# A planner's weights for VectorE work beside an attention stream: 99 pairs of quarter tiles become 103

## Chip, cores, metric

One NeuronCore of one Trainium2 chip runs the whole kernel. The metric is the device time of one execution in microseconds; the kernel before is given as the median of three runs, and one further execution was profiled.

## The reference, cut to what matters

The kernel computes two branches on the same input and mixes them with a gate per row:

```python
g = sigmoid((x * gate_w).sum(-1, keepdims=True))       # x: 1 x 2048 x 1024
a = state_space_branch(x)      # h[t] = Lam_bar * h[t-1] + Bu[t]; y = 2 Re(h C^T) + x * Dskip
qkv = x @ wqkv                 # 32 heads of 32
p = softmax(q @ k.T * 32 ** -0.5)
b = (p @ v) @ wo
out = g * a + (1 - g) * b
```

What matters here is the softmax: 32 heads x 2048 x 2048 exponentials have to be taken of scores that lie in PSUM.

## The kernel before, in words

**The stream.** The attention is cut into 8 groups of 4 heads, each group into 8 units of 256 queries, and each unit into 8 bursts (`BURSTS`): 512 bursts p = 0 to 511, unit U = p // 8. A burst (`burst`, L1613) is 8 score matmuls on TensorE (L1625), which fill two PSUM tiles of 128 x 1024, and two exponentials on ScalarE, `exp(0)` and `exp(1)`, one per tile (L1644). There are three such PSUM tiles, used in turn. The exponentials of a burst are multiplied with V some bursts later (`pv`, L1728) and summed in one PSUM bank, called "O". When the last burst of a unit has been summed, in burst 8U + 9, `normalize` (L1735) has VectorE take the reciprocal of the sums (L1741) and scale the result (L1742), and only then may the next unit's sums start in that bank. Everything else (projections, the state space branch, the output projection) is cut into chains of matmuls that are fed to TensorE, four to a burst ("dense" work), each chain ending with an evacuation by VectorE.

**The quarter tiles.** In some bursts ScalarE takes only 768 of the 1024 columns of the second tile (L1641), and VectorE takes the other 256. VectorE copies them scaled out of PSUM (`x_in`, L1634, 128x256). Two bursts make a pair, and for a pair VectorE then runs three steps of a polynomial over 128x512 (L1668, L1669, L1665, listed in `x_ops`, L1654); GpSimd turns the result into bf16 bits (`x_p`, L1666), and TensorE multiplies that with V (`x_pv`, L1695; its matmuls are L1707). `X_PLAN` (L937) lists where pairs lie. A unit with two pairs has them in its bursts (0, 2) and (4, 6); a unit with one pair has it in (0, 4). `x_plan` (L1648) sets when the result is multiplied, in `x_when`: in burst 8U + 7 for a pair (0, 2), in burst 8U + 9 for the others. I call that burst the due burst. The matmuls L1707 stand in TensorE's queue behind the values of earlier bursts and in front of that burst's dense matmuls and of all score matmuls of later bursts.

**The planner.** All queues are in order, and their order is written when the program is built. For each burst, `build` (L1753) keeps a model of VectorE's clock, `dve_t`, and a limit for the burst. The loop from L1926 on fills the room up to the limit with steps of three lists: `xbg` (the steps of pairs), `bg` (the state space items: 8 tensor_tensor and two scans each, `item_ops`, L1343) and `bg2` (tables and folds). It tries every number i of pair steps, j of item steps and k of table steps that fit, takes the best value, and issues the first step of that choice. `mixed` (L1672) says how long a choice takes and which step leads: it changes lists where it can, since a step right behind one of its own list costs `DEP` more. Before the change the value is

```python
v = (u + (0.3 * i if ended is not None else 9.0 * i) + 0.05 * sum(x[0] for x in bs[:j]), i, j, k, lead)
```

with u the time that the choice takes, and `ended` set where a dense chain ends in this burst. So in a burst without an evacuation, pair steps come first whenever they fit. If the steps of a pair are not all issued when its due burst comes, `values` (L1831) calls `x_flush` (L1689), which issues them there.

Of the kernel before, what the change touches and what calls it, by code (L numbers as in the profile page):

```python
# [927 lines left out]
PE_HEAD = 0.86  # L928
# [5 lines left out]
W_AT = (38, 0, 17)  # L934

X_AT = ((0, 2), (4, 6), (0, 4))
X_PLAN = (64, 72, 80, 88, 92, 96, 100, 104, 108, 112, 116, 120, 124, 128, 132, 136, 144, 152, 160, 168, 172, 176, 180, 184, 188, 192, 200, 208, 216, 224, 228, 232, 236, 240, 244, 248, 252, 256, 260, 264, 268, 272, 276, 280, 284, 288, 292, 296, 300, 304, 308, 312, 316, 320, 324, 328, 332, 336, 344, 348, 352, 356, 360, 364, 368, 372, 376, 380, 384, 388, 392, 396, 400, 404, 408, 412, 416, 420, 424, 428, 432, 436, 440, 444, 448, 452, 456, 460, 464, 468, 472, 476, 480, 484, 488, 492, 496, 500, 504)  # L937
X_COLS = 256
F_TS, F_ST = 1.32, 1.24
DEP = 0.12  # L940
I_MM = 0.6
X_LAST = 0.615
U_LAG, U_AHEAD = 3, 32
LATE, LATE0 = 0.35, 0.15
X_A = SCALE * math.log2(math.e) * 65536.0
X_LO = -127.0 * 65536.0
E3, E2, E1, E0 = 0.0780245226404788, 0.2260671649, 0.6958335355, 0.9999252185627155
# [13 lines left out]
class FastPath:  # L961
# [381 lines left out]
    def item_ops(self, j, ch, n):  # L1343
# [9 lines left out]
        def tt(c, o, a, b, op, r, w, d=0.0):  # L1353
            ops.append((c, d, lambda: dve(lambda e: e.tensor_tensor(o, a, b, op), r, w)))
        two = lambda ap: ap.unsqueeze(1).to_broadcast([128, 2, 512])
        tt(I_MM, ht[:], ub[s], two(er), ALU.mult, [u0, u1, Et], k[0:2])
        tt(I_MM, tq[:], ub[s], two(ei), ALU.mult, [u0, u1, Et], k[2:4])
        ops.append((0.0, 0.0, lambda: self.used_u(n)))
        tt(0.61, ut[:, 0, :], t[0], t[3], ALU.add, [k[0], k[3]], [("ut", 0)], DEP)
        tt(0.61, ut[:, 1, :], t[1], t[2], ALU.subtract, k[1:3], [("ut", 1)])  # L1360
# [7 lines left out]
        k = [("tq", 0), ("tq", 1), ("ut", 0), ("ut", 1)]  # L1368
        tt(I_MM, tq[:], ht[:], two(er), ALU.mult, [("ht", 0), ("ht", 1), Et], k[0:2], DEP)
        tt(I_MM, ub16[:, :, 0:512], ht[:], two(ei), ALU.mult, [("ht", 0), ("ht", 1), Et], k[2:4])  # L1370
        (h0, w0), (h1, w1) = self.hp_at(ch, j, 0), self.hp_at(ch, j, 1)
        hw = ["warm"] if ch == 0 and j == 0 else []
        if ch == 1 and j == 0:
            hw = ["fX", "fY", "m_c"] + self.EFtok + ["gp0", "gp1"]
        tt(0.345, h0, t[0], t[3], ALU.subtract, [k[0], k[3]], w0 + hw, DEP)
        tt(0.345, h1, t[2], t[1], ALU.add, k[1:3], w1 + hw)
# [236 lines left out]
    def burst(self, B):  # L1613
# [17 lines left out]
        if mine is not None:  # L1631
            b, n = mine
            s = sl[1]
            first = self.dve(lambda e: e.tensor_scalar(self.xi[:, b % 2, X_COLS * n:X_COLS * (n + 1)], ps[:, 2 * s + 1, 512 - X_COLS:512], X_A, X_LO, ALU.mult, ALU.max),  # L1634
                             [("S", s)], [("xi", b % 2, n)], "x_in")
# [18 lines left out]
    def x_ops(self, b):  # L1654
# [8 lines left out]
        def last():  # L1663
# [3 lines left out]
            self.x_done.add(b)  # L1667
        return [(0.61, DEP, lambda: self.dve(lambda e: e.scalar_tensor_tensor(xq[:], lo, E2 / E3 * w, lo, ALU.add, ALU.mult), i2, ["xq"], "x_q")),  # L1668
                (0.61, DEP, lambda: self.dve(lambda e: e.scalar_tensor_tensor(xq[:], xq[:], E1 / E3 * w * w, lo, ALU.add, ALU.mult), ["xq"] + i2, ["xq"], "x_q")),  # L1669
                (X_LAST, DEP, last)]  # L1670

    def mixed(self, xs, bs, ts):  # L1672

        rest = {"x": list(xs), "b": list(bs), "t": list(ts)}
        t, lane, lead = 0.0, self.lane, ""
        while True:
            some = [s for s in "xbt" if rest[s]]
            if not some:
                return t, lead
            s = next((s for s in some if s != lane), some[0])  # L1680
            if rest["b"] and rest["b"][0][0] == 0.0:
                s = "b"
            c, d = rest[s].pop(0)
            lead = lead or s
            if c > 0:
                t += c + (d if s == lane else 0.0)
                lane = s

    def x_flush(self):  # L1689
        c, d, f = self.xbg.pop(0)  # L1690
        f()
        self.dve_t += c + (d if self.lane == "x" else 0.0)
        self.lane = "x"
# [59 lines left out]
    def build(self):  # L1753
# [45 lines left out]
        outs, k = [], 0  # L1799
# [9 lines left out]
        t0, period = 0.0, PERIOD  # L1809
        for p in range(first, NBURST):  # L1810
# [3 lines left out]
            if p > first:  # L1814
                t0 += period
            if p % 4 == 0 and p in X_PLAN:
                one = p % 8 == 0 and p + 4 not in X_PLAN and p < NBURST - 8
                self.x_plan(p // 8, X_AT[2 if one else p // 4 % 2])
# [3 lines left out]
            period = PERIOD - (0.17 if p - 1 in self.x_of else 0.0)  # L1822
            if p in self.x_of:
                self.dve_t = max(self.dve_t, t0 + 0.45) + 0.4
                b, n = self.x_of[p]
                if n == 1:
                    self.xbg += self.x_ops(b)
                self.lane = "x"
            q0, q1 = self.quarters[p]

# [31 lines left out]
            if not wo1 and not cs and cur is None and self.c_left[3] == 0:  # L1862
                wo1 = True
                for a in range(7):
                    j = a if a < 3 else a - 3
                    x = [("cT", 0, j), ("cTf", 0, j, 0), ("cTf", 0, j, 1)]
                    if a in (3, 4, 5):
                        x = [("bT", a - 3)] + [("hp", 8, k) for k in (2 * a - 6, 2 * a - 5)]
# [11 lines left out]
            ended = None  # L1880
            while used < quota:
                if cur is None:
# [4 lines left out]
                    elif not last:  # L1887
                        nxt = proj[g + 1]
                        left = 64 - pg
                        need = 2 * len(nxt)  # L1890
                        u_ok = c_ok = False
                        if us:
                            ch, n, ri, dn = us[0]
# [16 lines left out]
                wt, f = cur.pieces.pop(0)  # L1910
# [3 lines left out]
                if not cur.pieces:  # L1914
                    ended = cur
# [4 lines left out]
            if behind:  # L1920
                values()
            log.append((p, ended.tag if ended else (cur.tag if cur else None), used, round(self.dve_t - t0, 2), len(self.bg) + len(self.bg2)))
            limit = t0 + period + PE_HEAD
            if ended is not None:
                limit = dense_end + (LATE if behind else LATE0 if period > 1.8 else 0.0)
            while self.xbg or self.bg or self.bg2:  # L1926
                now = max(self.dve_t, t0 + 0.3)
                room = limit - now + 1e-9
                xs, bs = [], []
                for c, d, f in self.xbg:  # L1930
                    if c == X_LAST and self.x_out != len(self.x_done):
                        break
                    xs.append((c, d))
                    if c == X_LAST:
                        break
                for c, d, f, n in self.bg:
                    if not ((n in self.tabled or not self.bg2) and self.item_ready(n)) or sum(x[0] for x in bs) > room:
                        break
                    bs.append((c, d))
                ts = [(c, 0.0) for c, f in self.bg2[:8]]  # L1940
                if not bs and not xs and not ts:
                    break
                best = None
                for i in range(len(xs) + 1):
                    for j in range(len(bs) + 1):
                        if self.mixed(xs[:i], bs[:j], [])[0] > room:
                            break
                        for k in range(len(ts) + 1):
                            u, lead = self.mixed(xs[:i], bs[:j], ts[:k])
                            if u > room:  # L1950
                                break
                            v = (u + (0.3 * i if ended is not None else 9.0 * i) + 0.05 * sum(x[0] for x in bs[:j]), i, j, k, lead)
                            if best is None or v > best:
                                best = v
                lead = best[4]
                if not lead:
                    break
                if lead == "x":
                    c, d, f = self.xbg.pop(0)
                elif lead == "b":  # L1960
                    c, d, f, n = self.bg.pop(0)
                else:
                    (c, f), d = self.bg2.pop(0), 0.0
                f()
                if c > 0:
                    self.dve_t = now + c + (d if self.lane == lead else 0.0)
                    self.lane = lead
# [189 lines left out]
```

## Time and profile before

| what | value |
|---|---|
| time, median of 3 runs (lowest to highest) | 925.74 us (924.91 to 925.8) |
| the profiled execution's own time | 925.63 us |
| its span, first to last instruction | 923.9 us |
| TensorE clock granted | 0.999 |
| VectorE busy | 770.5 us (83%) |
| GpSimd busy | 86.4 us (9%) |
| ScalarE instructions L1641 (768 columns) | 198 |
| GpSimd steps L1666 | 99 |

"Busy" is the union of an engine's instructions. ScalarE's instructions overlap one another at their ends, so the time that one of them really takes from the stream is read from start to start in the timeline. In the view of waits a line reads "who waited <- for whom: us in total, times, longest". In a timeline a row is start, length, engine, line, operation, tiles, count; several like instructions are merged into one row.

### The profile page before, as it was taken

The page shows a single profiled execution, that of the slowest core. Times are in us where ns is not written, and L with a number is a line of the kernel's source. Part 1 is how long each engine was busy: PE and PEld are TensorE (multiplying, and loading weights), DVE is VectorE, ACT ScalarE, POOL GpSimd, SP SyncE. Part 2 cuts the span into 40 slices and gives each one's busy share as a digit, 9 for nine tenths or more (in the row PEclk, how much of TensorE's full clock was granted, in tenths as well). Part 3 has the DMA queues.
Part 4 walks back from the last instruction along what each step waited for, and adds up shares of the span by engine and source line. Part 5 has one row for each costly group of instructions (what it writes and reads, how often), then busy time and mean ns, then how long its engine had stood idle before and what let it go on. Part 6 is the DMA issues. An engine that isn't in the chain of part 4 may idle for free.

```text
span 923.9 us, 34036 instructions
## 1 busy us (share of the span) xinstructions
PE 901.5 (98%) x15316; PEld 503.1 (54%) x15316; DVE 770.5 (83%) x1345; ACT 905.7 (98%) x1034; POOL 86.4 (9%) x163
## 2 busy tenths in 40 slices
PE   8899999999999999999999999999999999999996
PEld 4555744556555565555655565555655655545553
DVE  2788989999989999999999999989998655676665
ACT  6999999999999999999999999999999999999996
POOL 2000001011000101010111110101001010000010
PEclk9999999999999999999999999999999999999999
DMA  9449767630564202242212621622001012534422
GB/s 199 86 101 150 105 116 146 139 83 16 104 118 100 65 20 72 75 97 53 41 41 77 127 50 25 133 65 67 20 22 48 21 60 69 185 85 129 114 62 75
DMA packets 170983, 77.70 MB, mean 84 GB/s; under 512 B 147280, under 2 KB 155472, under 8 KB 170832
## 3 DMA queue, kind: packets, MB, share of 16 engines
q1 hardware_dynamic: 168672, 74.94, 35.7%
q8 instruction: 121, 1.98, 0.9%
q10 hardware_dynamic: 2160, 0.53, 0.3%
q14 instruction: 30, 0.25, 0.1%
HBM read 25.18 MB, written 20.97 MB: 50 GB/s over the span
## 4 chain that ended last, share of the span: by engine, by line
PE 54%; ACT 36%; DVE 5%; SPq 1%; DMA 1%; issue 1%; POOL 0%; DVEq 0%
ACT f_pt L1644 29%; PE f_ps L1728 14%; PE f_ps L1625 11%; PE f_ps L1427 9%; PE f_ps L1505 8%; PE f_ps L1458 6%; PE f_ps L1446 5%; ACT f_pt L1641 5%; SPq L1063 1%; ACT f_cT L1644 1%; DVE f_ht L1363 1%; ACT f_Et L1644 1%; PE f_ps L1707 1%; DMA f_xT<-in_A_x_dram 1%; PE f_ps L1511 0%
## 5 line engine op out<-in xcount | busy, mean ns | idle before, releaser
L1644 ACT ACTIVATE f_pt<-f_ps 128x1024 bf16<-128x1024 f32 x746 | 718.2, 1086 | 2.7 <-PE f_ps L1625 2.3
L1728 PEld LDWEIGHTS f_ps<-f_V,f_pt 128*128 128x128 bf16 x7156 | 220.8, 96 | 96.1 <-issue 69.7
L1728 PE MATMUL f_ps<-f_V,f_pt 128*128 128x33 bf16 x7156 | 257.2, 178 | 0.6 <-ACT f_pt L1644 0.6
L1625 PE MATMUL f_ps<-f_Q,f_K 32*128 32x256 bf16 x4096 | 203.3, 273 | 9.0 <-ACT f_cT L1644 2.2
L1641 ACT ACTIVATE f_pt<-f_ps 128x768 bf16<-128x768 f32 x198 | 176.6, 892 | 0.0
L1625 PEld LDWEIGHTS f_ps<-f_Q,f_K 32*128 32x128 bf16 x4096 | 60.7, 92 | 146.8 <-ACT f_pt L1644 118.5
L1458 PE MATMUL f_ps<-f_xT,f_wb 128*128 128x512 bf16 x512 | 131.5, 379 | 1.3 <-DVE f_pf L1240 0.5
L1666 POOL TENSOR_SCALAR f_xp<-f_xq 128x512 int16<-128x512 f32 x99 | 66.9, 676 | 618.9 <-DVE f_xq L1665 418.5
L1427 PE MATMUL f_ps<-f_xT,f_wb 128*128 128x512 bf16 x464 | 119.3, 379 | 0.4 <-DVE f_Q L1434 0.3
L1634 DVE TENSOR_SCALAR f_xi<-f_ps 128x256 int32<-128x256 f32 x198 | 83.4, 421 | 15.9 <-PE f_ps L1625 11.6
L1363 DVE TENSOR_TENSOR_SCAN f_ht<-f_pf,f_init,f_ut 128x512 bf16<-128x512 f32 x64 | 81.1, 1279 | 0.0
L1505 PE MATMUL f_ps<-f_cT,f_hp 128*128 128x512 bf16 x272 | 74.5, 379 | 0.1
L1669 DVE SCALAR_TENSOR_TENSOR f_xq<-f_xq,f_xi 128x512 f32<-128x512 f32 x99 | 68.5, 692 | 3.3
L1668 DVE SCALAR_TENSOR_TENSOR f_xq<-f_xi 128x512 f32<-128x512 uint16 x99 | 68.5, 692 | 3.3
L1665 DVE SCALAR_TENSOR_TENSOR f_xq<-f_xi,f_xq 128x512 f32<-128x512 int16 x99 | 68.2, 689 | 2.2
L1458 PEld LDWEIGHTS f_ps<-f_xT,f_wb 128*128 128x128 bf16 x512 | 40.1, 96 | 40.3 <-issue 9.1
L1446 PE MATMUL f_ps<-f_wb,f_xT 128*128 128x128 bf16 x896 | 59.3, 219 | 0.0
L1427 PEld LDWEIGHTS f_ps<-f_xT,f_wb 128*128 128x128 bf16 x464 | 36.1, 96 | 35.9 <-issue 7.6
L1446 PEld LDWEIGHTS f_ps<-f_wb,f_xT 128*128 128x128 bf16 x896 | 50.4, 97 | 3.8 <-issue 3.8
L1462 DVE CAST f_ub<-f_ps 128x512 bf16<-128x512 f32 x64 | 44.0, 688 | 9.5 <-PE f_ps L1458 8.6
L1741 DVE RECIPROCAL f_rc<-f_ps 128x8 f32<-128x8 f32 x63 | 13.0, 207 | 40.0 <-PE f_ps L1707 34.5
L1536 PE MATMUL f_ps<-f_cT,f_OT 128*128 128x512 bf16 x156 | 44.7, 378 | 0.1
(149 smaller groups left out, 829.0 us busy)
## 6 DMA issues: line engine op xcount, KB each, us to landing
u_scratch<-f_ub SPq DMA_DIRECT2D x64, 128.0 KB, 2.0
f_ub<-u_scratch SPq DMA_DIRECT2D x32, 256.0 KB, 2.9
ag_scratch<-f_Ag SPq DMA_DIRECT2D x32, 256.0 KB, 2.2
f_hp<-ag_scratch SPq DMA_DIRECT2D x32, 256.0 KB, 3.0
f_wb<-in_B_wqkv_dram SPq DMA_DIRECT2D x21, 256.0 KB, 4.1
out_dram<-f_xT SPq DMA_DIRECT2D x16, 256.0 KB, 2.2
f_cT<-in_B_wo_dram SPq DMA_DIRECT2D x5, 256.0 KB, 5.5
f_OT<-f_On SPq DMA_TRANSPOSE x63, 2.5
```

What stands on the lines that cost most here:

```text
L1363: ops.append((1.2, 0.0, lambda ri=ri: dve(lambda e: e.tensor_tensor_scan(ht[:, ri, :], rr, ut[:, ri, :], self.init[:, ri, j:j + 1], ALU.mu ...
L1427: mms.append((1, lambda e, f, l, a=a, w=w: e.matmul(ps[:, bank, :], w[:, a, :], xT[:, a, 512 * ch:512 * (ch + 1)], start=f, stop=l), [tok] ...
L1446: m = e.matmul(ps[:, bank, 128 * q:128 * (q + 1)], xT[:, a, 128 * kt:128 * (kt + 1)], w[:, a, :], start=(a == 0), stop=(a == 7))
L1458: mms.append((1, lambda e, f, l, a=a: e.matmul(ps[:, 7, :], bT[:, (2 * n + ri) % 3, a, :], xT[:, a, 512 * ch:512 * (ch + 1)], start=f, sto ...
L1505: mms.append((1, lambda e, f, l, j=j, ri=ri, h=h: e.matmul(ps[:, 7, :], h[:, cols], cT[ri][:, j, 512 * cb:512 * (cb + 1)], start=f, stop=l ...
L1625: m = e.matmul(ps[:, 2 * sl[h // 2] + h % 2, 256 * kl:256 * (kl + 1)], K[32 * h:32 * h + 32, g % 2, 128 * kt:128 * (kt + 1)], Q[32 * h:32 ...
L1634: first = self.dve(lambda e: e.tensor_scalar(self.xi[:, b % 2, X_COLS * n:X_COLS * (n + 1)], ps[:, 2 * s + 1, 512 - X_COLS:512], X_A, X_LO ...
L1641: self.S.op("act", lambda e: e.activation(flat(self.tile[p]), flat(ps[:, 2 * s:2 * s + 2, :]), ACT.Exp, scale=SCALE), reads=[("S", s)], wr ...
L1644: self.act(lambda e: e.activation(self.tile[p], ps[:, 2 * s:2 * s + 2, :], ACT.Exp, scale=SCALE), [("S", s)], [("pt", p)], "exp")
L1668: return [(0.61, DEP, lambda: self.dve(lambda e: e.scalar_tensor_tensor(xq[:], lo, E2 / E3 * w, lo, ALU.add, ALU.mult), i2, ["xq"], "x_q") ...
L1669: (0.61, DEP, lambda: self.dve(lambda e: e.scalar_tensor_tensor(xq[:], xq[:], E1 / E3 * w * w, lo, ALU.add, ALU.mult), ["xq"] + i2, ["xq"] ...
L1728: m = e.matmul(ps[:, 6, o:o + 33], self.tile[p][:, h2, 256 * kl + 128 * qt:256 * kl + 128 * (qt + 1)], V[:, g % 2, 2 * i + kl, h, :], star ...
```

## The change

The diff, cut to its core (`X_PLAN` grows by the entries 84, 156, 164 and 220; nothing leaves it):

```diff
+X_SOON, X_LEFT = 0.0, 2
+RC_LATE = 0.25
...
             s = next((s for s in some if s != lane), some[0])
+            if self.hurry and rest["x"]:
+                s = "x"
             if rest["b"] and rest["b"][0][0] == 0.0:
...
                 if n == 1:
-                    self.xbg += self.x_ops(b)
+                    due = 8 * (p // 8) + (7 if p % 8 < 4 else 9)
+                    self.xbg += [(c, d, f, due) for c, d, f in self.x_ops(b)]
...
-            limit = t0 + period + PE_HEAD
+            limit = t0 + period + PE_HEAD + (RC_LATE if p + 1 in self.quarters and self.quarters[p + 1][1] % 32 == 0 else 0.0)
             if ended is not None:
                 limit = dense_end + (LATE if behind else LATE0 if period > 1.8 else 0.0)
...
+                left = next((n for n, x in enumerate(self.xbg) if x[0] == X_LAST), 0) + 1
+                soon = self.xbg and left > self.xbg[0][3] - p - X_LEFT
+                self.hurry = soon and self.xbg[0][3] - p <= 1
...
-                            v = (u + (0.3 * i if ended is not None else 9.0 * i) + 0.05 * sum(x[0] for x in bs[:j]), i, j, k, lead)
+                            w = sum(x[0] for x in xs[:i] + bs[:j] + ts[:k])
+                            v = (w + ((0.3 if ended is not None else 9.0) if soon else X_SOON) * i + 0.05 * sum(x[0] for x in bs[:j]), i, j, k, lead)
```

- **Four more pairs.** Units 10, 19, 20 and 27 had one pair in bursts (0, 4); they now have two, in (0, 2) and (4, 6).
- **Weights.** Each step now carries its due burst. With `left` steps of the first pair open, the extra weight of a pair step counts only where `left` is more than due - p - 2; elsewhere a pair step counts like any other. The value uses w, the plain sum of the costs, in place of u, which held the bubbles between steps of one list too.
- **Hurry.** In the burst ahead of the due burst (and in it), a pair step leads whatever ran just before.
- **The limit.** In the burst ahead of a unit's reciprocal (p = 8U + 8), if no chain ends there, the limit is 0.25 later.

No instruction is of a new kind. The matmul work and the number of exponentials stay as they are.

More of the change, by code (lines that the diff above doesn't have):

```diff
@@ L936 @@
 X_AT = ((0, 2), (4, 6), (0, 4))
-X_PLAN = (64, 72, 80, 88, 92, 96, 100, 104, 108, 112, 116, 120, 124, 128, 132, 136, 144, 152, 160, 168, 172, 176, 180, 184, 188, 192, 200, 208, 216, 224, 228, 232, 236, 240, 244, 248, 252, 256, 260, 264, 268, 272, 276, 280, 284, 288, 292, 296, 300, 304, 308, 312, 316, 320, 324, 328, 332, 336, 344, 348, 352, 356, 360, 364, 368, 372, 376, 380, 384, 388, 392, 396, 400, 404, 408, 412, 416, 420, 424, 428, 432, 436, 440, 444, 448, 452, 456, 460, 464, 468, 472, 476, 480, 484, 488, 492, 496, 500, 504)
+X_PLAN = (64, 72, 80, 84, 88, 92, 96, 100, 104, 108, 112, 116, 120, 124, 128, 132, 136, 144, 152, 156, 160, 164, 168, 172, 176, 180, 184, 188, 192, 200, 208, 216, 220, 224, 228, 232, 236, 240, 244, 248, 252, 256, 260, 264, 268, 272, 276, 280, 284, 288, 292, 296, 300, 304, 308, 312, 316, 320, 324, 328, 332, 336, 344, 348, 352, 356, 360, 364, 368, 372, 376, 380, 384, 388, 392, 396, 400, 404, 408, 412, 416, 420, 424, 428, 432, 436, 440, 444, 448, 452, 456, 460, 464, 468, 472, 476, 480, 484, 488, 492, 496, 500, 504)
 X_COLS = 256
@@ L1689, in x_flush @@
     def x_flush(self):
-        c, d, f = self.xbg.pop(0)
+        c, d, f, due = self.xbg.pop(0)
         f()
@@ L1929, in build @@
                 xs, bs = [], []
-                for c, d, f in self.xbg:
+                for c, d, f, due in self.xbg:
                     if c == X_LAST and self.x_out != len(self.x_done):
@@ L1958, in build @@
                 if lead == "x":
-                    c, d, f = self.xbg.pop(0)
+                    c, d, f, due = self.xbg.pop(0)
                 elif lead == "b":
```

## The prediction

> **What bounds the kernel now.** I read the page first: its span and busy shares, then the two groups of exponentials.
>
> ```profile
> span 923.9 us, 34036 instructions
> PE 901.5 (98%) x15316; PEld 503.1 (54%) x15316; DVE 770.5 (83%) x1345; ACT 905.7 (98%) x1034; POOL 86.4 (9%) x163
> L1644 ACT ACTIVATE f_pt<-f_ps 128x1024 bf16<-128x1024 f32 x746 | 718.2, 1086 | 2.7 <-PE f_ps L1625 2.3
> L1641 ACT ACTIVATE f_pt<-f_ps 128x768 bf16<-128x768 f32 x198 | 176.6, 892 | 0.0
> ```
>
> PE and ACT both show 98%. The group rows show ACT waiting only 2.7 us in front of its 746 main instructions, and not at all in front of the 198 short ones. So ACT is the steady bound, with PE beside it. The waits say which of the two waits for the other:
>
> ```profile
> PEld f_ps L1625 <- ACT f_pt L1644: 118.5, 308, 1.0
> DVE f_rc L1741 <- PE f_ps L1707: 34.5, 38, 1.8
> PEld f_ps L1707 <- POOL f_xp L1666: 2.4, 4, 0.7
> ```
>
> PE waits 118.5 us for ACT before it writes new scores, so in most bursts PE has time to spare. The second row is the gap in front of the reciprocal: VectorE stands idle there, about 0.9 us each (34.5 / 38). The third row is small, but it is the one place where a late quarter tile holds PE's queue: four times, up to 0.7 us. What such a tile is worth on ACT is read from start to start in ACT's timeline, here for a unit with one pair (20) and one with two (21):
>
> ```profile
> 299.65 0.81 ACT L1641 ACTIVATE f_pt<-f_ps 128x768 bf16<-128x768 f32 x1
> 300.36 6.52 ACT L1644 ACTIVATE f_pt<-f_ps 128x1024 bf16<-128x1024 f32 x7
> ...
> 313.72 0.98 ACT L1641 ACTIVATE f_pt<-f_ps 128x768 bf16<-128x768 f32 x1
> 314.50 2.95 ACT L1644 ACTIVATE f_pt<-f_ps 128x1024 bf16<-128x1024 f32 x3
> 317.23 0.93 ACT L1641 ACTIVATE f_pt<-f_ps 128x768 bf16<-128x768 f32 x1
> 317.97 2.94 ACT L1644 ACTIVATE f_pt<-f_ps 128x1024 bf16<-128x1024 f32 x3
> 320.69 0.91 ACT L1641 ACTIVATE f_pt<-f_ps 128x768 bf16<-128x768 f32 x1
> 321.41 2.95 ACT L1644 ACTIVATE f_pt<-f_ps 128x1024 bf16<-128x1024 f32 x3
> 324.13 0.93 ACT L1641 ACTIVATE f_pt<-f_ps 128x768 bf16<-128x768 f32 x1
> 324.86 2.95 ACT L1644 ACTIVATE f_pt<-f_ps 128x1024 bf16<-128x1024 f32 x3
> 327.61 0.91 ACT L1641 ACTIVATE f_pt<-f_ps 128x768 bf16<-128x768 f32 x1
> ```
>
> Three full tiles take 317.23 - 314.50 = 2.73 us, 0.91 each. A short one takes 0.78, 0.74, 0.72 and 0.73 in the four places (0.71 in unit 20).
>
> **Term 1, the four pairs.** Each pair turns two full tiles into short ones. What is new in a unit are the places of bursts 2 and 6: 0.91 - 0.74 and 0.91 - 0.73, together 0.35 us. Four units make **-1.4 us**. Its ends: with the worst place (0.78) 8 x 0.13 = 1.0, with the best (0.71) 8 x 0.20 = 1.6.
>
> VectorE pays for them with two reads of PSUM and three steps a pair:
>
> ```profile
> L1634 DVE TENSOR_SCALAR f_xi<-f_ps 128x256 int32<-128x256 f32 x198 | 83.4, 421 | 15.9 <-PE f_ps L1625 11.6
> L1665 DVE SCALAR_TENSOR_TENSOR f_xq<-f_xi,f_xq 128x512 f32<-128x512 int16 x99 | 68.2, 689 | 2.2
> 690.00:713.00 23.00, 22.50 (x382) 12.10 (x381) 20.70 (x37) 22.44 (x27) 2.47 (x4) 1.00 0.22 54
> 713.00:736.00 23.00, 23.00 (x451) 15.31 (x448) 15.23 (x28) 23.00 (x28) 1.85 (x3) 1.00 0.06 17
> ```
>
> That is 2 x 0.42 + 3 x 0.69 = 2.9 us a pair, 11.6 us in all. (The steps L1668 and L1669 have the shape of L1665.) None of it stands on ACT's path. What hides it is the state space work, which fills VectorE up to 713 us (20.70 of 23 us busy) and then ends (15.23). 11.6 us more move that end back, less what the wider limit gains: at most 0.25 in each of the units 8 to 48, 41 x 0.25 = 10 us. I cost this at nothing. If the cover were gone, the last chunk of matmuls that needs the state space work would come up to 11.6 us later, in TensorE slots that are filled with projections meanwhile; as each is dense work in an existing slot, only the lack of a filler would cost. The new reads of PSUM themselves must be done before ACT's short tile. I take them as free too; if VectorE is behind, their price is what the late one of unit 20 has: it ends at 299.62, and the short tile starts at 299.65, so that the two full tiles from 297.60 on take 2.05 us where 1.82 is normal: 0.23 lost.
>
> ```profile
> 297.60 2.08 ACT L1644 ACTIVATE f_pt<-f_ps 128x1024 bf16<-128x1024 f32 x2
> ...
> 299.20 0.42 DVE L1634 TENSOR_SCALAR f_xi<-f_ps 128x256 int32<-128x256 f32 x1
> ```
>
> Eight new ones at that price would be 2 us, and this is the upper end.
>
> **Term 2, the late steps.** The four waits of PE for POOL look alike. This is the one at burst 288, in order of time, with a punctual one of unit 20 at the end:
>
> ```profile
> 523.29 0.42 DVE L1634 TENSOR_SCALAR f_xi<-f_ps 128x256 int32<-128x256 f32 x1
> 523.62 0.68 DVE L1354 TENSOR_TENSOR f_tq<-f_ht,f_Et 128x1024 bf16<-128x1024 bf16 x1
> 524.22 0.69 DVE L1665 SCALAR_TENSOR_TENSOR f_xq<-f_xi,f_xq 128x512 f32<-128x512 int16 x1
> 524.81 0.37 PE L1728 MATMUL f_ps<-f_V,f_pt 128*128 128x33 bf16 x8
> 524.93 2.03 ACT L1644 ACTIVATE f_pt<-f_ps 128x1024 bf16<-128x1024 f32 x2
> 524.99 0.62 POOL L1666 TENSOR_SCALAR f_xp<-f_xq 128x512 int16<-128x512 f32 x1 [1.95 <-DVE f_xq L1665]
> 525.66 0.27 PE L1707 MATMUL f_ps<-f_V,f_xp 128*128 128x33 bf16 x4 [0.49 <-POOL f_xp L1666]
> ...
> 527.18 1.02 ACT L1644 ACTIVATE f_pt<-f_ps 128x1024 bf16<-128x1024 f32 x1 [0.22 <-PE f_ps L1625]
> ...
> 300.06 0.37 PE L1728 MATMUL f_ps<-f_V,f_pt 128*128 128x33 bf16 x8
> 300.28 0.26 PE L1707 MATMUL f_ps<-f_V,f_xp 128*128 128x33 bf16 x4
> ```
>
> The pair's last step was left for the burst ahead of its due burst. There an item step (f_tq) went in front of it, because the planner changes lists where it can. The matmuls L1707 start 0.85 us behind the values' first matmul, against 0.22 in the punctual row: 0.63 late. The dense chain and the next scores stand behind them, and ACT's two tiles from 524.93 take 2.25 us where 1.82 is normal. So a late step is on the path with most of its length; four make the 2.4 us of the waits row.
>
> The change makes such a step lead. It would start at 523.62 instead of 524.22, 0.60 earlier, and if POOL followed as quickly, L1707 would be 0.03 late and the whole 2.4 us would go. But now f_tq runs right behind the step, beside POOL, and the trace has that case:
>
> ```profile
> 169.78 0.68 DVE L1354 TENSOR_TENSOR f_tq<-f_ht,f_Et 128x1024 bf16<-128x1024 bf16 x1
> 169.94 0.99 POOL L1666 TENSOR_SCALAR f_xp<-f_xq 128x512 int16<-128x512 f32 x1 [1.01 <-DVE f_xq L1665]
> ...
> L1666 POOL TENSOR_SCALAR f_xp<-f_xq x99: 617/618/1591, 139.9 to 906.8; 128x512 int16<-128x512 f32 x99
> ```
>
> Beside f_tq the POOL step takes 0.99 us instead of 0.62, and up to 1.59 elsewhere. Then a hurried step saves only 0.60 - 0.37 = 0.23 us, and four save 0.9. The Trainium skill (GPSIMD Engine Reference, section 8, Key points) speaks against the change in the same sense: GpSimd and VectorE share SBUF interfaces, and a VectorE instruction that reads two SBUF tensors or runs in a 2-port mode gets in GpSimd's way. The trace agrees (0.99 against 0.62 us beside an operation with two SBUF inputs); if the rule holds at all four places, term 2 is the 0.9, not the 2.4.
>
> Whether a last step still falls there depends on a new order of all VectorE work from burst 84 on. For the second pair of a unit the weights hardly change: three steps are left three bursts ahead of the due burst, and 3 > 3 - 2, so they weigh at once as before. For a first pair the weight starts one burst later than before. So I expect about as many late steps, cheaper ones, or fewer. I take the middle of 0.9 and 2.4, **-1.6 us**; the ends are -2.4 and, with as many late steps more, the slower rival below.
>
> **Term 3, the limit.** In busy units VectorE now runs up to 0.25 us into the gap in front of the reciprocal. Where the gap is 0.9 us, this costs nothing. The tightest case has no gap at all:
>
> ```profile
> 202.67 0.20 DVE L1741 RECIPROCAL f_rc<-f_ps 128x8 f32<-128x8 f32 x1
> 202.91 0.42 DVE L1742 SCALAR_TENSOR_TENSOR f_On<-f_ps,f_rc 128x256 bf16<-128x256 f32 x1
> ...
> 203.69 0.36 PE L1728 MATMUL f_ps<-f_V,f_pt 128*128 128x33 bf16 x8
> ```
>
> The scaled result is done at 203.33 and the bank is needed at 203.69, so 0.36 us are left there; 0.25 more still fit, with 0.11 over for the hand-over. The price lies between 0 and, if every one of 41 units lost 0.1, 4 us. I take **+0.2**, near the row, since the planner's steps are 0.6 or 1.2 long and seldom fill the last tenth. Queued behind the reciprocal on VectorE are the scaling, an evacuation and the next read of PSUM; they would shift by the same 0.25.
>
> **Sum.** Against the profiled execution's 925.63 (span 923.9 and 1.7 around it): 925.63 - 1.4 - 1.6 + 0.2 = **922.8 us**. The median of the runs, 925.74, is 0.11 above that execution; I leave it at 922.8.
>
> **Rivals.** The bound for "no change" is 0.2%, 1.85 us, about what a measurement of this kernel can tell; so faster is below 923.9 and slower above 927.6.
> - *All late steps go:* no pair ends in the burst ahead of its due burst. 925.63 - 1.6 - 2.4 - some tenths of the 2.7 us idle = 921.2. For it: the step leads there, and the limit has grown by 0.25. Against it: the POOL row.
> - *The pairs alone:* late steps are moved to other units and cost what they did, 925.63 - 1.4 + 0.2 = 924.4; this is also what comes out if "hurry" does not do what it says. For it: the weights in bursts with an evacuation are the same as before (0.3), and there a scan of 1.2 beats a step.
> - *Reciprocals late:* all of term 3's upper end eats the gain: 925.63 - 1.4 - 1.6 + 4 = 926.6.
> - *Slower, more late steps:* the first pair's later weight pushes its last step into the second pair's time, so that two steps of a second pair are left for the burst ahead of the due burst, or a step is followed by an operation that holds POOL for its longest, 1.59. Each such pair costs about 0.63 + 0.3 = 0.9 us at L1707. It decides the sign when their sum passes 1.4 + 2.4 + 1.85 = 5.7 us, from some six or seven such pairs among about forty in the busy stretch: 928.2 with seven.
>
> **Chances.** Forecast 0.45; all gone 0.17; pairs alone 0.20; reciprocals late 0.06; slower 0.12. Faster holds the first two, 0.62; same the next two, 0.26; slower 0.12. The range goes from 920.8 (term 1 at 1.6, term 2 at 2.4, and 0.8 of the idle) to 926.0, inside the case of late reciprocals; it leaves out the slower rival and the end of that case.
>
> **What would show it.** Term 1: 206 rows of L1641, and units 10, 19, 20 and 27 shorter by 0.35 us. Term 2: PE's wait for POOL at L1707 falls from 2.4 us, and where it stays, the POOL step is longer than 0.62. Term 3: reciprocals wait less for PE than 34.5 us and no L1728 waits for L1742. It is wrong if L1707 waits more than four times at 0.6, or if L1641 shows idle time in front for L1634.

## The result and the profile after

The changed kernel takes 923.76 us (median of 17 runs, 923.08 to 924.54), the kernel before 925.6 (17 runs, 924.65 to 925.94). The ratio is 0.9982, 95% interval 0.9975 to 0.9988: faster by 1.7 us going by the ratio and by 1.84 going by the medians. My bound for "no change" was 0.2%, 1.85 us, so this is at its edge; that it is faster is clear. The profiled execution took 923.76, so the two profiled executions are 1.87 us apart. The line numbers have moved: L1646 and L1643 are the full and the short exponentials, L1667 the last step of a pair, L1668 GpSimd's step, L1711 the pair's matmuls, L1732 the values, L1745 and L1746 the reciprocal and the scaling.

Lines of the changed kernel's page, then some of its waits (who waited <- for whom: us, times, longest), and the line of GpSimd's step before. Here and below only the rows that matter are shown, of timelines too:

```profile
span 921.9 us, 33840 instructions
...
L1646 ACT ACTIVATE f_pt<-f_ps 128x1024 bf16<-128x1024 f32 x738 | 711.9, 1082 | 3.2 <-PE f_ps L1627 3.0
L1643 ACT ACTIVATE f_pt<-f_ps 128x768 bf16<-128x768 f32 x206 | 183.0, 889 | 0.0
L1668 POOL TENSOR_SCALAR f_xp<-f_xq 128x512 int16<-128x512 f32 x103 | 82.8, 804 | 598.7 <-DVE f_xq L1667 423.8
```

```profile
PEld f_ps L1627 <- ACT f_pt L1646: 117.6, 302, 1.0
...
DVE f_rc L1745 <- PE f_ps L1711: 36.2, 38, 1.8
...
PEld f_ps L1711 <- POOL f_xp L1668: 1.7, 3, 0.9
PEld f_ps L1732 <- DVE f_On L1746: 1.5, 7, 0.2
...
DVE f_ht L1356 <- DMA f_ub<-u_scratch: 1.1, 1, 1.1
```

```profile
L1666 POOL TENSOR_SCALAR f_xp<-f_xq 128x512 int16<-128x512 f32 x99 | 66.9, 676 | 618.9 <-DVE f_xq L1665 418.5
```

ScalarE is still the bound, with 206 short tiles. The waits at L1711 went from four (2.4 us) to three (1.7 us), not to none, and GpSimd's step grew from 676 to 804 ns on average. The last of the waits is new: VectorE waits 1.1 us for a load.

**Where the 1.87 us came from.** The gain has two parts that I had foreseen, the tiles of the four pairs and the late steps. A third part appeared in the opening, and a wait for a load took about half of the foreseen gain away.

*The pairs.* ScalarE's timeline at the new short tiles (bursts 2 and 6) of units 10, 19 and 20:

```profile
163.26 0.93 ACT L1643 ACTIVATE f_pt<-f_ps 128x768 bf16<-128x768 f32 x1
164.04 2.90 ACT L1646 ACTIVATE f_pt<-f_ps 128x1024 bf16<-128x1024 f32 x3
...
288.46 0.93 ACT L1643 ACTIVATE f_pt<-f_ps 128x768 bf16<-128x768 f32 x1
289.30 2.86 ACT L1646 ACTIVATE f_pt<-f_ps 128x1024 bf16<-128x1024 f32 x3
...
295.48 0.83 ACT L1643 ACTIVATE f_pt<-f_ps 128x768 bf16<-128x768 f32 x1
296.22 2.88 ACT L1646 ACTIVATE f_pt<-f_ps 128x1024 bf16<-128x1024 f32 x3
...
302.72 0.83 ACT L1643 ACTIVATE f_pt<-f_ps 128x768 bf16<-128x768 f32 x1
303.56 2.85 ACT L1646 ACTIVATE f_pt<-f_ps 128x1024 bf16<-128x1024 f32 x3
...
309.68 0.89 ACT L1643 ACTIVATE f_pt<-f_ps 128x768 bf16<-128x768 f32 x1
310.37 2.94 ACT L1646 ACTIVATE f_pt<-f_ps 128x1024 bf16<-128x1024 f32 x3
```

From start to start: 0.78, 0.84, 0.74, 0.84, 0.69 us. The other place of unit 10 and the two of unit 27 are 0.73, 0.78 and 0.73. Against 0.91 of a full tile the eight save 1.15 us. The two of 0.84 are those of burst 2 in units 19 and 20.

*The late steps.* Seven last steps still lie in the burst ahead of their due burst (due 177, 241, 273, 281, 297, 321, 369). Each leads now. Behind four of them (177, 281, 321, 369) VectorE runs the reciprocal next; there GpSimd's step takes 0.62 us and the four cost hardly anything. The dearest is the one of burst 241:

```profile
438.41 0.68 DVE L1667 SCALAR_TENSOR_TENSOR f_xq<-f_xi,f_xq 128x512 f32<-128x512 int16 x1
439.01 1.28 DVE L1365 TENSOR_TENSOR_SCAN f_ht<-f_pf,f_init,f_ut 128x512 bf16<-128x512 f32 x1
439.18 1.52 POOL L1668 TENSOR_SCALAR f_xp<-f_xq 128x512 int16<-128x512 f32 x1 [3.07 <-DVE f_xq L1667]
439.55 0.37 PE L1732 MATMUL f_ps<-f_V,f_pt 128*128 128x33 bf16 x8
440.76 0.27 PE L1711 MATMUL f_ps<-f_V,f_xp 128*128 128x33 bf16 x4 [0.84 <-POOL f_xp L1668]
442.31 1.02 ACT L1646 ACTIVATE f_pt<-f_ps 128x1024 bf16<-128x1024 f32 x1 [0.70 <-PE f_ps L1627]
```

The step itself came in time. A scan runs right behind it, and beside the scan GpSimd's step takes 1.52 us; L1711 starts 1.21 us behind the values where 0.22 is punctual, and ScalarE stands idle for 0.70. The two other waits (273, 297) have f_tq behind the step and a GpSimd step of 0.99. Less waiting at L1711 is worth 2.4 - 1.7 = 0.7 us.

*The opening.* Before and after, the starts of bursts 40 and 41 on ScalarE (two full tiles lie between):

```profile
84.95 1.94 ACT L1644 ACTIVATE f_pt<-f_ps 128x1024 bf16<-128x1024 f32 x2
87.08 1.94 ACT L1644 ACTIVATE f_Et<-f_ps 128x1024 bf16<-128x1024 f32 x2 [0.19 <-PE f_ps L1625]
```

```profile
84.60 1.94 ACT L1646 ACTIVATE f_pt<-f_ps 128x1024 bf16<-128x1024 f32 x2
86.42 1.95 ACT L1646 ACTIVATE f_Et<-f_ps 128x1024 bf16<-128x1024 f32 x2
```

2.13 us became 1.82. In the kernel before, an item step stood between the scaling and the evacuation of a projection, and TensorE waited for that evacuation. Burst 58 gains as much. Together this is 0.6 us, which I had not foreseen; 0.2 of it is lost again in bursts 60 to 64.

*The load.* At burst 68 of the changed kernel:

```profile
138.04 0.69 DVE L1356 TENSOR_TENSOR f_ht<-f_ub,f_Et 128x1024 bf16<-128x1024 bf16 x1 [1.13 <-DMA f_ub<-u_scratch]
138.13 3.77 ACT L1646 ACTIVATE f_pt<-f_ps 128x1024 bf16<-128x1024 f32 x4
...
140.46 0.69 DVE L1464 CAST f_ub<-f_ps 128x512 bf16<-128x512 f32 x1
...
141.50 0.81 PE L1460 MATMUL f_ps<-f_xT,f_wb 128*128 128x512 bf16 x3 [1.27 <-DVE f_ub L1464]
...
142.69 1.94 ACT L1646 ACTIVATE f_pt<-f_ps 128x1024 bf16<-128x1024 f32 x2 [0.79 <-PE f_ps L1627]
```

The first pair's steps no longer come first there; an item step does, and its input has not landed. VectorE stands for 1.13 us, the evacuation behind it is late, the chain behind the evacuation starts 1.27 late, and ScalarE idles 0.79. From start to start its four tiles take 142.69 - 138.13 = 4.56 us here, where four full tiles elsewhere take 3.63: 0.93 is lost, in burst 70.

*The sum.* Subtract the start of every burst on ScalarE in the one profiled execution from that in the other. Most bursts between 71 and 510 take the same time in both within 0.03 us, so the differences can be put to places. They add up to the 1.97 us between the two spans:

| where | changed less before, us |
|---|---|
| bursts 0 to 39 | -0.35 |
| bursts 40 and 58, the earlier evacuation | -0.60 |
| bursts 59 to 65 | +0.20 |
| burst 70, behind the load | +0.93 |
| units 10, 19, 20 and 27, the new pairs | -1.16 |
| the four late steps of before (185, 289, 329, 385) gone | -2.68 |
| the late steps 241, 273 and 297 of the changed kernel | +1.87 |
| everything else | -0.18 |

The first line is no gain of the change. VectorE's order is the same in both up to 70.8 us (burst 33), and nearly all of the 0.35 arises ahead of that. Two runs below that share the order of the kernel before there reach burst 40 at 84.84 (hurry alone) and 86.42 us (the step ahead of the read) where the kernel before has 84.95. What makes the opening vary by over a microsecond from execution to execution is not shown.

### The profile page after: what moved, and what is told of

The parts are those of the page before. It is cut to its first block, busy times and chain, and to the rows that moved or that the text cites. A ratio compares the mean times of both kernels' runs of the same rounds, so it can differ in the third digit from the quotient of the medians.

```text
span 921.9 us, 33840 instructions
## 1 busy us (share of the span) xinstructions
PE 882.3 (96%) x15095; PEld 503.8 (55%) x15316; DVE 769.6 (83%) x1365; ACT 903.8 (98%) x1034; POOL 101.9 (11%) x167
## 4 chain that ended last, share of the span: by engine, by line
PE 53%; ACT 30%; DVE 13%; issue 2%; DMA 1%; POOL 0%; DVEq 0%; SPq 0%
ACT f_pt L1646 23%; PE f_ps L1732 12%; PE f_ps L1627 10%; PE f_ps L1507 8%; PE f_ps L1429 8%; PE f_ps L1460 6%; PE f_ps L1448 5%; ACT f_pt L1643 5%; DVE f_xi L1636 3%; DVE f_ht L1365 2%; ACT f_cT L1646 1%; DVE f_ub L1464 1%; DVE f_Ag L1520 1%; PE f_ps L1711 1%; DVE f_xq L1670 1%
## 5 line engine op out<-in xcount | busy, mean ns | idle before, releaser
L1646 ACT ACTIVATE f_pt<-f_ps 128x1024 bf16<-128x1024 f32 x738 | 711.9, 1082 | 3.2 <-PE f_ps L1627 3.0
L1732 PEld LDWEIGHTS f_ps<-f_V,f_pt 128*128 128x128 bf16 x7140 | 221.7, 96 | 94.7 <-issue 65.9
L1732 PE MATMUL f_ps<-f_V,f_pt 128*128 128x33 bf16 x7140 | 256.9, 178 | 0.1
L1643 ACT ACTIVATE f_pt<-f_ps 128x768 bf16<-128x768 f32 x206 | 183.0, 889 | 0.0
L1668 POOL TENSOR_SCALAR f_xp<-f_xq 128x512 int16<-128x512 f32 x103 | 82.8, 804 | 598.7 <-DVE f_xq L1667 423.8
L1460 PE MATMUL f_ps<-f_xT,f_wb 128*128 128x512 bf16 x448 | 117.7, 379 | 9.0 <-DVE f_ub L1464 1.7
L1429 PE MATMUL f_ps<-f_xT,f_wb 128*128 128x512 bf16 x406 | 106.7, 379 | 4.1 <-issue 0.4
L1636 DVE TENSOR_SCALAR f_xi<-f_ps 128x256 int32<-128x256 f32 x206 | 86.8, 421 | 25.8 <-PE f_ps L1627 21.5
L1671 DVE SCALAR_TENSOR_TENSOR f_xq<-f_xq,f_xi 128x512 f32<-128x512 f32 x103 | 71.0, 689 | 2.5
L1670 DVE SCALAR_TENSOR_TENSOR f_xq<-f_xi 128x512 f32<-128x512 uint16 x103 | 70.7, 686 | 2.5 <-POOL f_xp L1668 0.7
L1667 DVE SCALAR_TENSOR_TENSOR f_xq<-f_xi,f_xq 128x512 f32<-128x512 int16 x103 | 70.8, 687 | 1.9
L1507 PE MATMUL f_ps<-f_cT,f_hp 128*128 128x512 bf16 x240 | 67.6, 379 | 2.5 <-DVE f_Ag L1520 0.5
L1745 DVE RECIPROCAL f_rc<-f_ps 128x8 f32<-128x8 f32 x63 | 13.0, 206 | 40.5 <-PE f_ps L1711 36.2
L1356 DVE TENSOR_TENSOR f_ut<-f_ht,f_tq 128x512 f32<-128x512 bf16 x64 | 43.0, 691 | 0.6
```

What stands on the lines that cost most here:

```text
L1429: mms.append((1, lambda e, f, l, a=a, w=w: e.matmul(ps[:, bank, :], w[:, a, :], xT[:, a, 512 * ch:512 * (ch + 1)], start=f, stop=l), [tok] ...
L1460: mms.append((1, lambda e, f, l, a=a: e.matmul(ps[:, 7, :], bT[:, (2 * n + ri) % 3, a, :], xT[:, a, 512 * ch:512 * (ch + 1)], start=f, sto ...
L1507: mms.append((1, lambda e, f, l, j=j, ri=ri, h=h: e.matmul(ps[:, 7, :], h[:, cols], cT[ri][:, j, 512 * cb:512 * (cb + 1)], start=f, stop=l ...
L1643: self.S.op("act", lambda e: e.activation(flat(self.tile[p]), flat(ps[:, 2 * s:2 * s + 2, :]), ACT.Exp, scale=SCALE), reads=[("S", s)], wr ...
L1646: self.act(lambda e: e.activation(self.tile[p], ps[:, 2 * s:2 * s + 2, :], ACT.Exp, scale=SCALE), [("S", s)], [("pt", p)], "exp")
L1668: self.pool(lambda e: e.tensor_scalar(bits, xq[:], X_K, 128.0 * (E0 + 126.0), ALU.mult, ALU.add), ["xq"], p2, "x_p")
```

## The experiments

My theory: ScalarE sets the pace; what the plan does to VectorE matters only through the last steps of pairs (by when they come and by what runs on VectorE beside GpSimd's step) and through the one wait for the load. The rivals were that hurry gives all of its 0.6 us, that late steps are made good, that the pairs buy nothing beside a busy TensorE, that the load's wait is absorbed, and that the limit acts by itself. In every run the planned order says how many last steps are late; that is a list read off before the run. The four pairs by themselves could not be tried: with the old weights or the old limit the state space work ends too late for the chains that need it, and no order comes out.

**Hurry alone** (the kernel before, with this only):

```diff
             s = next((s for s in some if s != lane), some[0])
+            if self.hurry and rest["x"]:
+                s = "x"
```

> The kernel before with one part of the change: in the burst ahead of its due burst a pair step leads. The planned order keeps the same four late last steps (due bursts 185, 289, 329, 385), each now right behind the read of PSUM. Theory (GpSimd's step collides with the item step that now runs beside it): the last step is 0.6 us earlier, GpSimd's step takes 0.99 instead of 0.62, TensorE's wait at the pair's matmuls falls from about 0.6 to about 0.4 each, time 925.6 - 0.9 = 924.7. Rival (no collision): GpSimd's step stays at 0.62, TensorE does not wait for it at all, time 925.6 - 2.4 = 923.2.

Measured: 925.3 against 926.06 us, ratio 0.9992 (0.9983 to 1.0001), that is 0.8 us less. The place that the prediction quoted, due burst 289, and the waits of this run:

```profile
523.41 0.68 DVE L1667 SCALAR_TENSOR_TENSOR f_xq<-f_xi,f_xq 128x512 f32<-128x512 int16 x1
524.01 0.68 DVE L1356 TENSOR_TENSOR f_tq<-f_ht,f_Et 128x1024 bf16<-128x1024 bf16 x1
524.17 0.99 POOL L1668 TENSOR_SCALAR f_xp<-f_xq 128x512 int16<-128x512 f32 x1 [1.34 <-DVE f_xq L1667]
524.60 0.37 PE L1732 MATMUL f_ps<-f_V,f_pt 128*128 128x33 bf16 x8
525.23 0.27 PE L1711 MATMUL f_ps<-f_V,f_xp 128*128 128x33 bf16 x4 [0.26 <-POOL f_xp L1668]
```

```profile
PEld f_ps L1711 <- POOL f_xp L1668: 1.5, 4, 0.4
```

All four GpSimd steps take 0.99, as worked out: the step leads, and f_tq takes most of that back. The wait fell from 2.4 to 1.5. The time alone doesn't settle it (its interval reaches 1.0001); the rows do. Apart from these four places VectorE's order is that of the kernel before, and from start to start ScalarE gains 0.23 us at each of them, 0.9 in all.

**The step ahead of the read.** In place of leading behind the read of PSUM, the late step goes ahead of it, so that GpSimd's step runs beside the read:

```diff
+            while p % 8 == 0 and self.xbg and self.xbg[0][3] - p <= 1:
+                self.x_flush()
             second = self.burst(p)
```

> As hurry alone (99 pairs, the same four late last steps), but the late last step is put ahead of the read of PSUM of that burst, so that GpSimd's step runs beside that read, which takes its input from PSUM, and not beside the item step with two inputs in SBUF. Theory (it is the item step that stretches GpSimd's step): GpSimd's four steps take 0.62 again and TensorE does not wait for them; the read of PSUM is up to 0.6 us later, which may cost ScalarE some 0.2 us at each of the four places; 925.6 - 2.8 + 0.8 = 923.6. Rival (the step is long because of its place in the burst, not because of its neighbour): 0.99 as before, 924.7.

Measured: 923.79 against 925.82 us, ratio 0.9974 (0.9963 to 0.9985). The same place:

```profile
524.22 0.68 DVE L1667 SCALAR_TENSOR_TENSOR f_xq<-f_xi,f_xq 128x512 f32<-128x512 int16 x1
524.82 0.42 DVE L1636 TENSOR_SCALAR f_xi<-f_ps 128x256 int32<-128x256 f32 x1
524.99 0.62 POOL L1668 TENSOR_SCALAR f_xp<-f_xq 128x512 int16<-128x512 f32 x1 [1.01 <-DVE f_xq L1667]
525.16 0.99 DVE L1356 TENSOR_TENSOR f_tq<-f_ht,f_Et 128x1024 bf16<-128x1024 bf16 x1
...
525.97 0.26 PE L1711 MATMUL f_ps<-f_V,f_xp 128*128 128x33 bf16 x4
```

GpSimd's step is 0.62 again, at all four places, and no L1711 waits in this run. Together with the changed kernel, where a step in the place of hurry alone takes 0.62 ahead of a reciprocal and 0.99 ahead of f_tq, this shows that the neighbour stretches the step, not its place. The later read cost less than I had allowed: from start to start ScalarE gains 2.6 us at the four places, 0.1 short of what it gains there in the next run, in which no step is late. The Trainium skill (GPSIMD Engine Reference, section 8, Key points) names this contention between GpSimd and VectorE operations with two SBUF inputs; both runs agree, 0.99 beside f_tq and 0.62 beside a read of PSUM.

**None late.** The changed kernel, with the weight of 9 two bursts ahead of the due burst even where a chain ends:

```diff
-((0.3 if ended is not None else 9.0) if soon else X_SOON)
+((0.3 if ended is not None and self.xbg[0][3] - p > 2 else 9.0) if soon else X_SOON)
```

> The changed kernel with one number moved: from two bursts ahead of the due burst on, a pair step weighs 9 also where a dense chain ends (0.3 before), so that the planned order holds no last step in the burst ahead of its due burst or later; 103 pairs as in the changed kernel. Theory (three late steps still cost the changed kernel about 0.83 + 0.55 + 0.4 us on ScalarE): 923.8 - 1.8 = 922.0, and no wait of TensorE for GpSimd. Rival (what a late step holds up is made good later, so it is not on the path): 923.8.

Measured: 922.52 against 926.06 us, ratio 0.996 (0.9947 to 0.9974). The changed kernel's ratio is 0.9982, so taking its late steps away is worth about 2 us, as worked out, and the rival falls: at bursts 241, 273 and 297 ScalarE is 1.85 us shorter from start to start. No L1711 waits. This is the fastest version here, with the one of the wider limit below, which can't be told from it.

**None late, without the four pairs** (84, 156, 164 and 220 taken out of `X_PLAN`):

> As the run with no late step, without the four added pairs (99 pairs, none late). Only the pairs differ between the two. Theory: the four pairs are worth 1.4 us, so this takes 1.4 more than the run with no late step, about 923.4. Rival (TensorE is the bound in the units that got them, so shorter exponentials buy nothing there): at most 0.7 more.

Measured: 923.74 us, ratio 0.9973 (0.9963 to 0.9984): 1.2 us more than with the pairs. The two intervals overlap, so the time alone shows little; the starts on ScalarE do more. Between the two profiled executions units 10, 19, 20 and 27 differ by 0.37, 0.22, 0.12 and 0.37 us and unit 21 by another 0.06, together 1.1, about what the eight tiles gave in the timeline above (1.15). The rival, at most 0.7, falls.

**The same 99 pairs, early weights as before** (up to burst 71):

```diff
-                soon = self.xbg and left > self.xbg[0][3] - p - X_LEFT
+                soon = self.xbg and (p < 72 or left > self.xbg[0][3] - p - X_LEFT)
```

> As the 99 pairs with none late, and up to burst 71 pair steps weigh as in the kernel before, so that at burst 68 VectorE runs a pair's steps while the load of the state space item is under way. The changed kernel stands still there for 1.1 us behind an item step that waits for that load, and ScalarE shows 0.8 us idle. Theory (that wait is on the path): 0.9 us less than the 99 pairs with none late, about 922.5, and no wait of VectorE for that load. Rival (absorbed): the same time.

Measured: 922.91 us, ratio 0.9965 (0.9951 to 0.9979), 0.8 us less than the run before it. VectorE no longer waits for the load of f_ub, while the two runs before it wait 1.4 and 1.3 us there. The intervals overlap here too, but the starts on ScalarE are clear: burst 70 takes 1.81 us, as in the kernel before, and 2.90 in the run before this one. So the wait is on the path, with 1.1 us. The new order gives part of it back elsewhere: burst 80 is 0.25 us longer, and burst 326 by 0.43, behind an evacuation that waits for a store.

```profile
588.04 0.69 DVE L1464 CAST f_ub<-f_ps 128x512 bf16<-128x512 f32 x1 [1.61 <-DMA u_scratch<-f_ub]
589.09 0.81 PE L1460 MATMUL f_ps<-f_xT,f_wb 128*128 128x512 bf16 x3 [0.61 <-DVE f_xi L1636]
590.28 1.02 ACT L1646 ACTIVATE f_pt<-f_ps 128x1024 bf16<-128x1024 f32 x1 [0.24 <-PE f_ps L1627]
```

That the time comes out near my 0.9 is thus in part luck.

**The limit wider still** (`RC_LATE` 0.40 in the version with none late):

> As the run with no late step (103 pairs), with the limit in front of the reciprocal 0.40 later instead of 0.25; no last step is late in the planned order. The tightest units of the changed kernel have 0.05 to 0.2 us left between the scaled result and the next sums. Theory (0.25 costs next to nothing, what is beyond it is paid one to one where it is used): up to 0.15 us in some ten to twenty of the busy units, 0.5 to 2 us more than the run with no late step, and waits of TensorE for the scaled result of 0.1 and more. Rival (the bank has room for 0.4 as well): the same time.

Measured: 922.68 against 925.82 us, ratio 0.9966 (0.9954 to 0.9978). The waits of TensorE for the scaled result, first with 0.25, then with 0.40:

```profile
PEld f_ps L1732 <- DVE f_On L1746: 2.7, 13, 0.2
```

```profile
PEld f_ps L1732 <- DVE f_On L1746: 2.7, 13, 0.2
```

They are the same, and each is no longer than the 0.21 that a load of weights behind scores shows in the kernel before too ("issue"). The run says less than I had hoped, though. VectorE's order differs from that of the run with 0.25 in the opening and around unit 20 alone, and from burst 141 on every burst takes the same time in both within 0.03 us. So the wider limit was hardly used, and what 0.40 would cost where it is used stays open. My 0.5 to 2 took some ten to twenty units to use it.

**The changed kernel without hurry** (`self.hurry = False`):

> The changed kernel without hurry. The planned order has seven last steps in the burst ahead of their due burst (due bursts 177, 241, 273, 305, 329, 353, 377), none of them put first. Theory (a late step that does not lead costs about 0.7 us, as in the kernel before): 7 x 0.7 = 4.9 us where the changed kernel pays about 1.8, so 923.8 + 3.1 = 926.9, slower than before in spite of the four pairs; TensorE waits seven times for GpSimd at the pair's matmuls. Rival (hurry matters little, late steps are few): 923.8.

Measured: 931.45 against 925.82 us, ratio 1.0059 (1.0046 to 1.0072): slower than before, as expected, and by more than I had worked out. A late step of this run, and its waits:

```profile
326.75 0.41 DVE L1636 TENSOR_SCALAR f_xi<-f_ps 128x256 int32<-128x256 f32 x1
327.08 1.28 DVE L1365 TENSOR_TENSOR_SCAN f_ht<-f_pf,f_init,f_ut 128x512 bf16<-128x512 f32 x1
328.27 0.67 DVE L1667 SCALAR_TENSOR_TENSOR f_xq<-f_xi,f_xq 128x512 f32<-128x512 int16 x1
```

```profile
PEld f_ps L1711 <- POOL f_xp L1668: 7.9, 7, 1.3
```

In five of the seven a scan now stands in front of the step, 1.28 us where f_tq took 0.68; in the two others f_tq stands in front and one more item step behind, so that GpSimd's step takes 1.00. A wait is 1.1 us, not 0.7, and 7.9 - 1.7 = 6.2 us more are waited than in the changed kernel. The two profiled executions are 929.72 - 923.76 = 5.96 us apart, which the waits explain. The medians are 7.7 apart: the profiled execution was the fastest of this kernel's five, and what made the others slower is not shown.

**The later limit alone** (the kernel before with `RC_LATE` 0.25, nothing else):

> The kernel before with the later limit alone (0.25), old weights, no hurry, 99 pairs. The planned order then has nine late last steps where the kernel before has four. Theory (the number of late steps sets the time): five more at 0.7 us, 925.6 + 3.5 = 929.1. Rival (the wider limit lets VectorE catch up and costs nothing): 925.6 or less.

Measured: 929.59 against 925.82 us, ratio 1.0039 (1.0026 to 1.0052).

```profile
PEld f_ps L1711 <- POOL f_xp L1668: 7.0, 7, 1.2
```

Of nine late steps seven cost something, 1.0 each: in six of them f_tq stands in front of the step and another item step behind it, in one a scan in front. So 3.5 was close partly by luck. Three more late steps cost something than before, not five, each cost 1.0 and not 0.7 (7.0 - 2.4 = 4.6 us more), and the opening gave 0.4 back. The part of the change that was to use an idle gap makes the kernel slower by itself, by moving steps of pairs.

## Why the prediction came out as it did

The time lies 1.0 us above my 922.8, inside the range. The bound, the path of a late step and the collision on GpSimd were right. The sizes were not all, and that I am no further off is partly luck: the load and the late steps made it about 1.8 us dearer than I had said, and the opening, of which I had said nothing, gave 0.75 back, 0.35 of it by chance.

- **Term 1** (-1.4): measured -1.15. The step that failed is taking 0.74 us for burst 2 from unit 21. In units 19 and 20 those tiles take 0.84. TensorE runs the state space output chains (L1507) beside them; that these are the reason is not shown, since burst 6 of unit 19 has them too and takes 0.74. The result is inside the ends 1.0 to 1.6.
- **VectorE's work at nothing:** it held in the units of the new pairs. What hides it is a narrow cover, though: without the new weights or the later limit no order comes out at all.
- **Term 2** (-1.6): measured -0.7 by the waits, -0.8 from start to start, just short of the lower of the two values, 0.9 and 2.4, that I took the middle of. "About as many late steps, cheaper ones" was half right: they are seven instead of four, and cheaper (1.7 us in all instead of 2.4). The 0.23 us for a hurried step beside f_tq is what the run with hurry alone shows. The failed step is taking the middle between the two ends as the value: a new order draws new neighbours, and one scan beside GpSimd cost more than the old late step did.
- **Term 3** (+0.2): ScalarE shows next to nothing of it with 0.25. The two signs that I had named did not come: the reciprocals wait 36.2 us for TensorE, not less than 34.5 (28.3 with none late), and TensorE waits seven times for the scaled result, 0.2 each, which costs ScalarE 0.07 at burst 362 and nothing that can be seen elsewhere. What I missed is that the limit acts outside units 8 to 48 too: I took the order to be new from burst 84 on, and it is new from burst 33 on. It moves an evacuation forward in the opening (-0.6 at bursts 40 and 58, +0.2 behind them; the run with the limit alone starts burst 41 earlier in the same way, 1.82 us behind burst 40). The limit's real price is indirect: alone it raised the late steps from four to nine.
- **Missing term:** the load at burst 68, +0.9. I asked what the new weights do to the pair's steps, and not what runs in their place. The steps had been covering a load.
- **The slower rival** has the right mechanism, and the run without hurry is that case: seven steps at 1.1 us. I asked for six or seven at 0.9.

## What to carry to other kernels

When a planner's weights change, count the events that the path is made of (here last steps that come late) in the planned order, since one part of such a change can be slower by itself and still be what makes the whole fit. Ask of each step that is moved away what it was covering, a load above all. And where a step is handed from VectorE to GpSimd on the path, look at which operation VectorE runs next. When a change is worth a microsecond or two, compare two profiled executions burst by burst, from start to start on the engine that sets the pace: here that told places of 0.2 us apart where the totals could not.

## What the runs showed of the hardware that was not expected

The contention between the two engines goes by who is first. Where f_tq (two SBUF inputs, 0.68 us alone) started first, GpSimd's step took 0.99 in place of 0.62; where GpSimd's step started first, f_tq took 0.99 and the step its 0.62, in the run with the step ahead of the read. Behind a scan of 1.28 us GpSimd's step took 1.52. A read of PSUM beside it cost it nothing. The whole trace of the changed kernel fits: 33 of GpSimd's 103 steps take 0.73 us or more (10 of 99 before, which is why the mean grew), 32 of them beside a VectorE operation with two tensors in SBUF that is already running and one beside a running tensor_scalar (L1321); the 70 others take 0.62.
